# Signs of the weights through a two-slope activation, and written-out step lists, in an attention + feed-forward kernel on one core

## The chip, the core and the metric

The kernel runs on one core of one Trainium2 chip. The core has a matrix engine (PE), a vector engine (DVE), a scalar or activation engine (ACT), a third elementwise engine (POOL) and a queue of its own for issuing transfers (SP). Each of them executes its own instructions in program order and waits on semaphores of the others. The metric is the device time of one execution in microseconds; lower is better. The kernel before takes 952.94 us, the median of three runs (951.0 to 953.82).

## The reference

There are 8 batches of 8 heads with 512 local and 32 global tokens of 64 features. Local queries see the 32 global keys and the local keys at most 32 positions away; global queries see everything. The result, 512 features a token, goes through a feed-forward layer of 2048 hidden features.

```python
s_g = scale * np.matmul(q_g, k_all.transpose(0, 1, 3, 2))
out_g = np.matmul(sm(s_g), v_all)
s_ll = np.where(np.abs(pos[:, None] - pos[None, :]) <= 32, s_ll, -1e9)
a_l = sm(np.concatenate([s_lg, s_ll], axis=-1))
out_l = np.matmul(a_l, np.concatenate([v_g, v_l], axis=2))
x = np.concatenate([out_g, out_l], axis=2)   # then tokens x 512
h = x @ w_in                                 # 512 -> 2048
g = np.maximum(h, 0.0) + np.log1p(np.exp(-np.abs(h)))
out = g @ w_out                              # 2048 -> 512
```

## The kernel before

The weights lie in memory as 64-bit floats. Each of the 32 tiles (`wi0` to `wi15` of the first matrix, `wo0` to `wo15` of the second) arrives as two int32 words a number, `wiraw`/`woraw`, and passes three steps. **W** (`weight_mul`, L576, ACT) multiplies the high words, read as fp32, by 2^-112, which moves the exponent to fp32's bias. **B** or **b** (`weight_bits`, L581 to L583, DVE) shifts that word left by 3, puts the sign back and fills in three bits of the low word; B works in a PSUM bank (tag `a`), b in an SBUF tile. **H** or **h** (`weight_halves`, L588 on ACT and L589 on POOL for H, on DVE for h) splits the fp32 number into a high and a low fp32r half. The activations are split likewise (`xh`, `xl`, and `gh`, `gl`), and a product is three matmuls: high by high, high by low, low by high.

A feed-forward tile is 128 hidden features of a batch's 512 tokens, 16 tiles to a batch. `h` is 12 matmuls of 512 columns into one of two banks (tag `h`), written in two halves of 6. Then come Abs, Exp and Ln on ACT (L628 to L630), a max-and-add on DVE (`e`, L631), the cast `gh` on ACT (L634) and the difference `gl` on POOL (L635). `o` is 12 matmuls into four output banks, in two halves of 6.

Attention of batch 0 runs first, in eight groups of its heads, with its own layout: U steps in the lists below (scores `s`, sums, exps L200, diagonals, turned probabilities `t`, casts `p_..gh`/`p_..gl` L241 and L242, values `o`, and the split of x, L259 and L260). The global queries of batch 0 are two more groups (`s0g`, `t0g`, `p0g1gh` L284, `p0g1gl` L285, `o0g`). Later batches have four pairs of heads each, m = 4 to 31: scores `s_ps` (S with its mask added by PE matmuls and a copy on ACT L342, D with its mask added on DVE L340), maxima M (L343 to L401), products P on POOL or Q on DVE (L413, L415), exps E (L419), sums Z and R (`zt`, `rb`), values V (`v_ps`, and `xa` L466), X for the split. The `a` bank is used in turn by turned probabilities, B steps, `v_ps` and half of `s_ps`; the `h` banks also hold parts of `v_ps` and `s_ps` in steady batches.

The order on every engine is the order in which the program is written. Before, it comes from three tables: `START`, a list of steps for the time before the first feed-forward tile; `SLOTS`, four places of steps for each of batch 0's 16 tiles; and `S_AT`, `V_AT`, `PRE`, from which `later` and `moe_items` put the attention of the next batch between the tiles of the present one. Attention of batch b+1 thus runs among the feed-forward tiles of batch b; batch 7 has no attention beside it, and a last short pass (`GLOBAL` below) does the global tokens.

Of the kernel before, what the change touches and what calls it, by code (L numbers as in the profile page):

```python
# [8 lines left out]
F32 = mybir.dt.float32  # L9
# [4 lines left out]
ALU = mybir.AluOpType  # L14
# [17 lines left out]

M0 = 4
MLAST = 7
S_AT = (2, 4, 9, 11)
V_AT = (8, 15)
PRE = (3, 3)
START = (
# [4 lines left out]
)  # L43
SLOTS = (
    ('U65 B B M4 U66 H P41 P40', 'B', 'S50 H', 'W E41'),
    ('D51 E40 U93 W Z4 U94 B H', 'W', 'B B H', 'H M5 U95 W U96'),
    ('H', '', 'W', 'B R4 W'),
    ('', '', 'B', ''),
    ('W W B P51', 'B W', '', 'P50'),
    ('', 'E50', 'V4', 'B'),  # L50
    ('E51 H B W', '', 'Z5 S60', 'W h S61'),
    ('B B H W', 'W W B', 'h H', 'R5'),
    ('h', 'H', 'V5 M6', ''),
    ('', 'H W P60 D70', '', ''),
    ('B', '', 'D71', 'E60 P61 B H'),
    ('H B', 'E61 H M7 W', 'W W', 'P70 B Z6 W H'),
    ('H B', 'E70', '', 'H B R6 H'),
    ('', '', 'W P71', 'V6 B'),
    ('B h', '', 'H', ''),
    ('E71 Z7 W', '', 'B X0', 'H R7 X1 V7'),  # L60
)
GW = 76
W_PRE = 9
# [18 lines left out]
def moe_over_global_local_attention(  # L82
# [294 lines left out]
    def spread(mt):  # L377
        for a in range(1, 4):
            inorder(nc.gpsimd.tensor_copy(mt[0:32, GW * a:GW * a + GW], mt[32 * a:32 * a + 32, 0:GW]))
# [103 lines left out]
            if k < M:  # L483
                load_v(k)

    def step_of(o):

        kind, m, p = o[0], int(o[1:2] or 0), int(o[2:3] or 0)
        if kind in "SD":
            return [lambda: scores(m, p, kind == "D"), lambda: load(m + 1, p), *([lambda: spread(st["mt", m])] if p else [])]  # L490
        if kind == "V":
            return [lambda: values(m, a_banks(m)), lambda: values_out(m), lambda: load_v(m + 2)]
        if kind == "U":
            return [lambda: steps[m][0][p](*steps[m][1])]
        return {"M": [lambda: maxima(m), lambda: lift(m, 0), lambda: lift(m, 1)], "P": [lambda: probs(m, p, nc.gpsimd)],
                "Q": [lambda: probs(m, p, nc.vector)], "E": [lambda: exps(m, p)], "Z": [lambda: sums_first(m)],
                "R": [lambda: sums_rest(m)], "X": [lambda: split_x(1, m)], "K": [key_masks],
                "W": [weight_mul], "B": [lambda: weight_bits(True)], "b": [lambda: weight_bits(False)],
                "H": [lambda: weight_halves(nc.gpsimd)], "h": [lambda: weight_halves(nc.vector)]}[kind]

    def later():

        plan = {}

        def put(f, what, *fs):
            plan.setdefault((f // NF, f % NF, what), []).extend(fs)

        for f, slots in enumerate(SLOTS):
            for what, ops in zip(("pre", "act", "mid", "end"), slots):
                for o in ops.split():  # L510
                    put(f, what, *step_of(o))
        for m in range(MLAST + 1, M):
            b, i = divmod(m - 4, H // 2)
            at = NF * b + S_AT[i]
            put(at, "group", lambda m=m: scores_all(m), lambda m=m: spread(st["mt", m]))
            if m + 1 < M:
                put(at, "group", *[lambda m=m, p=p: load(m + 1, p) for p in range(NPC)])
            put(at + 1, "act", lambda m=m: maxima(m), *[lambda m=m, p=p: lift(m, p) for p in range(NPC)], lambda m=m: probs(m, 0, nc.gpsimd))
            put(at + 2, "act", lambda m=m: exps(m, 0), lambda m=m: probs(m, 1, nc.gpsimd))
            put(at + 3, "act", lambda m=m: exps(m, 1))  # L520
            if m % 2:
                at = NF * b + V_AT[i // 2]
                put(at - 1, "end", lambda m=m: sums_first(m))
                if i // 2:
                    put(at, "act", lambda b=b: split_x(b + 1, 0), lambda b=b: split_x(b + 1, 1))
                put(at, "act", lambda m=m: sums_rest(m))
                put(at, "group", lambda m=m: values_two(m - 1))
            else:
                put(at + 4, "act", lambda m=m: sums_first(m))
                put(at + 5, "act", lambda m=m: sums_rest(m))  # L530
        return plan

    halved = set()

# [38 lines left out]

    def abs_w(kind, k):
        hi = raws[kind, k][:, :, 1]
        note("act", nc.scalar.mul(hi.bitcast(F32), hi.bitcast(F32), DOWN))  # L576

    def bits_w(kind, k, r):
        t = raws.pop((kind, k))
        lo32, hi32 = t[:, :, 0], t[:, :, 1]  # L580
        note("dve", nc.vector.tensor_scalar(r, hi32, 3, None, op0=ALU.logical_shift_left))  # L581
        note("dve", nc.vector.scalar_tensor_tensor(r, hi32, -0x80000000, r, op0=ALU.bitwise_and, op1=ALU.bitwise_or))
        note("dve", nc.vector.scalar_tensor_tensor(lo32, lo32, 29, r, op0=ALU.logical_shift_right, op1=ALU.bitwise_or))  # L583
        return lo32.bitcast(F32)

    def halves_w(kind, k, r, engine):
# [10 lines left out]
    one = const.tile([P, 1], F32, name="one")  # L597
    nc.vector.memset(one, 1.0)

    def moe_items():  # L600


        tiles = [(b, f) for b in range(B) for f in range(NF)] + [(B, f) for f in range(NF // 2)]
        g, po, items = {}, {}, []

        def parts(b, f):

# [58 lines left out]
        halves = [(c, f, t) for c, f in tiles for t in range(0, 4 if c < B else 2, 2)]

        def second(i, at):
            c, f, t0 = halves[i]
            items.append((at, 2, 0, lambda: [opart(c, f, t) for t in (t0, t0 + 1)]))  # L670


        done, plan = 0, later()

        def run(fs):
            return lambda: [f() for f in fs]

        for i, (b, f) in enumerate(tiles):
            if f == 0 and b > 0:
                items.append((b, 0, 0, lambda b=b: [split_x(b, j) for j in range(4) if (b, j) not in halved]))  # L680
                second(done, b)
                done += 1
            w = 0 if b else 4 * f
            items.append((b, 2, w and w + 2, lambda b=b, f=f: hpart(b, f, (0, 1))))
            if (b, f, "pre") in plan:
                items.append((b, 0, 0, run(plan.pop((b, f, "pre")))))
            items.append((b, 2, w and w + 4, lambda b=b, f=f: (hpart(b, f, (2, 3)), act(b, f))))
            if (b, f, "act") in plan:
                items.append((b, 0, 0, run(plan.pop((b, f, "act")))))
            behind = 1 if ((b, f + 1) not in tiles and (b, f, 'group') not in plan) or (f == 0 and b > 0 and (b, 2, 'group') not in plan) else 2  # L690
            upto = halves.index(tiles[i - behind] + (0,)) + (2 if tiles[i - behind][0] < B else 1) if i >= behind else 0
            while done < upto:
                second(done, b)
                done += 1
                if (b, f, "mid") in plan:
                    items.append((b, 0, 0, run(plan.pop((b, f, "mid")))))
            if (b, f, "mid") in plan:
                items.append((b, 0, 0, run(plan.pop((b, f, "mid")))))
            if (b, f, "group") in plan:
                ahead = PRE[f in V_AT]  # L700
                for k in range(ahead - 2):
                    second(done, b)
                    done += 1
                items.append((b, 0, 0, run(plan.pop((b, f, "group")))))
                second(done, b)
                done += 1
            for what in ("max", "end"):
                if (b, f, what) in plan:
                    items.append((b, 0, 0, run(plan.pop((b, f, what)))))
        assert not plan, plan  # L710
        while done < len(halves):
            second(done, B)
            done += 1
        return items
# [55 lines left out]
    for o in START.split():
        for f in step_of(o):
            f()
    strict.append(1)
    items = moe_items()
    loads(W_PRE + 6)
    for b, size, w, it in items:
        if b == B - 1 and started:
            started.clear()  # L780
        it()
    assert wk[1] == len(order_w) and not todo and not done_bits
# [58 lines left out]
```

## Time and profile before

| | |
|---|---|
| median of three runs | 952.94 us |
| the profiled execution | 953.57 us, span 951.8 us |
| granted TensorE clock, mean | 0.995 |
| PE busy | 927.0 us, 97% |
| DVE, ACT, POOL busy | 589.9, 495.8, 452.4 us (62, 52, 48%) |
| PE's matmuls for h and o, of the chain that ended last | 37% and 37% of the span |

PE is busy nearly throughout, so the time is PE's work and the stretches in which it has none or runs at a lower clock. Both can be read from a table of windows: window less busy PE time is idle time; a granted clock below 1 stretches matmuls that count as busy.

### The profile page before, as it was taken

How to read it: one execution, taken by the hardware profiler on the slowest of the kernel's cores; microseconds unless marked ns; L12 is line 12 of the kernel's file. 1: busy time of each engine (PE TensorE's matmuls, PEld its weight loads, DVE VectorE, ACT ScalarE, POOL GpSimd, SP SyncE). 2: the span in 40 equal slices, each digit the busy share in tenths (PEclk: the TensorE clock that was granted, in tenths of full speed). 3: DMA queues.
4: the chain of work that ended last, by engine and by line, in shares of the span. 5: the costliest groups of instructions: out<-in, count | busy, mean ns of one | idle time of the engine just before them, and what ended most of it. 6: DMA issues, size and time to landing. Idle time of an engine off the chain costs nothing.

```text
span 951.8 us, 14719 instructions
## 1 busy us (share of the span) xinstructions
PE 927.0 (97%) x5465; PEld 766.2 (80%) x5468; DVE 589.9 (62%) x1197; ACT 495.8 (52%) x835; POOL 452.4 (48%) x672
## 2 busy tenths in 40 slices
PE   6899999999999999999999999999999999999997
PEld 4677786788888888888888888888888888888896
DVE  6889798667673767567684767466675757311211
ACT  5757666645364535634465535544455535544453
POOL 4346558445462727445462726444554636322221
PEclk9998999999999999999999999999999999999999
DMA  9546321120202121221211121211111010200000
GB/s 354 191 163 234 108 79 43 60 85 20 78 19 92 32 66 32 80 63 36 63 48 64 32 66 32 80 62 38 61 57 58 28 50 1 69 1 1 23 23 23
DMA packets 30697, 64.60 MB, mean 68 GB/s; under 512 B 7328, under 2 KB 7840, under 8 KB 30624
## 3 DMA queue, kind: packets, MB, share of 16 engines
q1 hardware_dynamic: 29888, 63.32, 20.0%
q8 instruction: 43, 0.70, 0.3%
q10 hardware_dynamic: 736, 0.33, 0.2%
q14 instruction: 30, 0.25, 0.1%
HBM read 54.20 MB, written 9.44 MB: 67 GB/s over the span
## 4 chain that ended last, share of the span: by engine, by line
PE 87%; DVE 4%; ACT 4%; POOL 2%; issue 2%; DMA 0%; ACTq 0%; POOLq 0%; DVEq 0%; SPq 0%
PE h L150 37%; PE o L150 37%; PE s_ps L150 6%; PE v_ps L150 5%; ACT e L200 1%; PE t L150 1%; PE s L150 1%; POOL wi L589 1%; DVE e L631 1%; DVE mt L343 1%; ACT e L630 1%; PE o0g L150 1%; DVE sums L197 1%; ACT e L629 1%; ACT e L628 0%
## 5 line engine op out<-in xcount | busy, mean ns | idle before, releaser
L150 PE MATMUL h<-xh,wi 128*128 128x512 f32 (+1 forms) x1152 | 342.1, 380 | 3.1 <-POOL wi L589 1.7
L150 PE MATMUL o<-wo,gh 128*128 128x512 f32 x1088 | 341.4, 395 | 0.2 <-POOL wo L589 0.2
L635 POOL TENSOR_TENSOR gl<-e,gh 128x512 fp32r<-128x512 f32 x136 | 175.4, 1290 | 317.5 <-ACT gh L634 228.0
L631 DVE SCALAR_TENSOR_TENSOR e<-h,e 128x512 f32<-128x512 f32 x136 | 92.9, 683 | 287.4 <-ACT e L630 281.1
L150 PEld LDWEIGHTS h<-xh,wi 128*128 128x128 f32 x1152 | 213.2, 189 | 45.8 <-POOL wi L589 2.5
L150 PEld LDWEIGHTS o<-wo,gh 128*128 128x128 f32 x1088 | 200.9, 188 | 44.4 <-POOL wo L589 0.5
L150 PE MATMUL h<-xl,wi 128*128 128x512 f32 (+1 forms) x576 | 218.3, 379 | 0.0
L150 PE MATMUL o<-wo,gl 128*128 128x512 f32 x544 | 211.8, 389 | 0.0
L628 ACT ACTIVATE e<-h 128x512 f32<-128x512 f32 x136 | 80.5, 592 | 227.5 <-PE h L150 189.7
L634 ACT CAST gh<-e 128x512 fp32r<-128x512 f32 x136 | 84.4, 621 | 131.8 <-DVE e L631 131.8
L150 PEld LDWEIGHTS h<-xl,wi 128*128 128x128 f32 x576 | 109.0, 189 | 20.4
L150 PEld LDWEIGHTS o<-wo,gl 128*128 128x128 f32 x544 | 102.3, 188 | 22.0
L413 POOL TENSOR_TENSOR s<-s,mb 128x768 f32<-128x768 f32 (+1 forms) x56 | 95.8, 1710 | 14.1 <-PE o L150 11.5
L630 ACT ACTIVATE e<-e,one 128x512 f32<-128x512 f32 x136 | 98.6, 725 | 4.4
L629 ACT ACTIVATE e<-e 128x512 f32<-128x512 f32 x136 | 86.0, 632 | 4.3
L419 ACT ACTIVATE s<-s 128x1024 f32<-128x1024 f32 x56 | 59.2, 1059 | 20.3 <-POOL s L415 20.3
L430 DVE TRANSPOSE_TENSOR_REDUCE zt<-s 128x32 f32<-128x1024 f32 x56 | 65.8, 1212 | 1.1 <-ACT s L419 1.1
L150 PE MATMUL s_ps<-raw 64*128 64x192 f32 (+2 forms) x672 | 63.5, 319 | 0.1
L150 PEld LDWEIGHTS s_ps<-raw 64*128 64x128 f32 x672 | 53.2, 187 | 9.8 <-issue 9.7
L368 DVE TRANSPOSE_TENSOR_REDUCE mt<-s 128x32 f32<-128x1024 f32 x48 | 56.7, 1219 | 0.0
L150 PEld LDWEIGHTS v_ps<-s,v 128*64 128x64 f32 x896 | 49.1, 137 | 8.8 <-issue 6.7
L150 PE MATMUL v_ps<-s,v 128*64 128x96 f32 (+3 forms) x896 | 54.1, 278 | 1.1 <-issue 1.1
(153 smaller groups left out, 833.2 us busy)
## 6 DMA issues: line engine op xcount, KB each, us to landing
raw<-in_qk SPq DMA_DIRECT2D x32, 352.0 KB, 3.0
v<-in_v SPq DMA_DIRECT2D x28, 384.0 KB, 3.2
raw<-in_qk SPq DMA_DIRECT2D x28, 368.0 KB, 3.7
wiraw<-in_w_in SPq DMA_DIRECT2D x16, 512.0 KB, 8.9
woraw<-in_w_out SPq DMA_DIRECT2D x16, 512.0 KB, 8.6
out<-ot SPq DMA_DIRECT2D x32, 256.0 KB, 2.1
v<-in_v SPq DMA_DIRECT2D x4, 512.0 KB, 8.7
raw<-in_qk SPq DMA_DIRECT2D x4, 416.0 KB, 8.3
```

What stands on the lines that cost most here:

```text
L150: order["pe"] = after(nc.tensor.matmul(*a, **k), "pe").ins
L197: keep("dve", nc.vector.tensor_reduce(t[:, 0, 0:n], ps, axis=AX.X, op=ALU.max))
L368: inorder(nc.vector.tensor_reduce(windows(mt, 4 + 16 * p, 36, 2, 16), st["s", m, p].rearrange("p h (b k) -> p h b k", k=32), axis=AX.X, op ...
L413: inorder(engine.tensor_tensor(sw, sw, pairs(mb, 352, mo, md, w), op=ALU.subtract))
L419: inorder(nc.scalar.activation(s, s, AF.Exp, scale=0.125))
L430: inorder(nc.vector.tensor_reduce(windows(zt, 4 + 16 * p, 36, 2, 16), st["s", m, p].rearrange("p h (b k) -> p h b k", k=32), axis=AX.X, op ...
L628: inorder(nc.scalar.activation(e, ph, AF.Abs))
L629: inorder(nc.scalar.activation(e, e, AF.Exp, scale=-1.0))
L630: inorder(nc.scalar.activation(e, e, AF.Ln, bias=one))
L631: inorder(nc.vector.scalar_tensor_tensor(e, ph, 0.0, e, op0=ALU.max, op1=ALU.add))
L634: inorder(nc.scalar.copy(gh, e))
L635: inorder(nc.gpsimd.tensor_tensor(gl, e, gh.bitcast(F32), op=ALU.subtract))
```

## The change

First, `abs_w` uses a parametric ReLU instead of a multiplication: the scale is 2^-112 as before, and negative words are multiplied by 2^32 besides. That puts a bit into them which the later shift by 3 moves to the sign's place. `bits_w` then needs two DVE instructions instead of three. Second, the tables and the two functions that read them are replaced by four lists: `OPENING` (batch 0's attention, the weights, batch 0's 16 tiles and batch 1's attention), `STEADY` for each of batches 1 to 6, `LAST` and `GLOBAL`. In them `h` is a tile's first half, `g` its second half and the activation, `o` two output rows; N is what H was. In the listing of the changed program line numbers are one higher through the attention and five or six higher from the weights' steps on.

```diff
-START = (
-    "U00 U10 U01 W U11 K U02 U12 U20 U03 b U04 H W U30 b U21 U31 U13 U22 U14 H W U05 "
...
-SLOTS = (
-    ('U65 B B M4 U66 H P41 P40', 'B', 'S50 H', 'W E41'),
...
+OPENING = (
+    "U00 K U10 U01 U11 U02 U12 W U20 b U03 U04 N W U30 U13 b U21 U22 U14 W U40 b U05 U23 U31 "
...
+STEADY = (
+    "x2 x3 o h g h g o h g o o o S0 o h g M0 P00 h o g P01 o E00 o "
+    "S1 E01 o h g M1 P10 h g E10 P11 o h Z0 o g o E11 o Z1 h R0 o g R1 o "
...
-        note("act", nc.scalar.mul(hi.bitcast(F32), hi.bitcast(F32), DOWN))
+        note("act", nc.scalar.activation(hi.bitcast(F32), hi.bitcast(F32), AF.Prelu, scale=DOWN, alpha=2.0 ** 32))
...
-        note("dve", nc.vector.tensor_scalar(r, hi32, 3, None, op0=ALU.logical_shift_left))
-        note("dve", nc.vector.scalar_tensor_tensor(r, hi32, -0x80000000, r, op0=ALU.bitwise_and, op1=ALU.bitwise_or))
-        note("dve", nc.vector.scalar_tensor_tensor(lo32, lo32, 29, r, op0=ALU.logical_shift_right, op1=ALU.bitwise_or))
+        note("dve", nc.vector.tensor_scalar(r, lo32, 29, None, op0=ALU.logical_shift_right))
+        note("dve", nc.vector.scalar_tensor_tensor(lo32, hi32, 3, r, op0=ALU.logical_shift_left, op1=ALU.bitwise_or))
...
+        def ff_first():
+            hpart(*tiles[count["h"]], (0, 1))
+            count["h"] += 1
+        def ff_second():
+            hpart(*tiles[count["g"]], (2, 3))
+            act(*tiles[count["g"]])
+            count["g"] += 1
+        def ff_out():
+            c, f, t0 = halves[count["o"]]
+            for t in (t0, t0 + 1):
+                opart(c, f, t)
+            count["o"] += 1
...
+    for o in OPENING.split():
+        if o == "h" and not strict:
+            strict.append(1)
+        step_of(o, 0)
+    for b in range(1, B - 1):
+        for o in STEADY.split():
+            step_of(o, b)
```

The lists move instructions on all engines. On PE, at the end of batch 0's own attention, the values of the second group of global queries (`o0g1`) stand before between the last half of `h0_1` and `h0_2`:

```order
L150 MATMUL h0_1_788<-xh0_3_674,wi1_308 128x512 x2
L150 MATMUL h0_1_788<-xl0_3_675,wi1_308 128x512
L150 MATMUL o0g1_884<-p0g1gh_830,v0_2_125 128x64 x4
L150 MATMUL o0g1_884<-p0g1gl_831,v0_2_125 128x64
L150 MATMUL o0g1_884<-p0g1gh_830,v0_3_135 128x64 x4
L150 MATMUL o0g1_884<-p0g1gl_831,v0_3_135 128x64
L150 MATMUL h0_2_902<-xh0_0_354,wi2_362 128x512 x2
```

and now:

```order
L151 MATMUL h0_1_761<-xl0_3_634,wi1_356 128x512
L151 MATMUL o0_0_858<-wo0_539,gh0_0_754 128x512 x2
L151 MATMUL o0_0_858<-wo0_539,gl0_0_755 128x512
L151 MATMUL o0_1_862<-wo0_539,gh0_0_754 128x512 x2
L151 MATMUL o0_1_862<-wo0_539,gl0_0_755 128x512
L151 MATMUL o0_2_866<-wo0_539,gh0_0_754 128x512 x2
L151 MATMUL o0_2_866<-wo0_539,gl0_0_755 128x512
L151 MATMUL o0_3_870<-wo0_539,gh0_0_754 128x512 x2
L151 MATMUL o0_3_870<-wo0_539,gl0_0_755 128x512
L151 MATMUL o0g1_874<-p0g1gh_820,v0_2_125 128x64 x4
```

The 12 output matmuls of tile 0, which stood behind `h0_2`, now stand ahead of `o0g1`.

On POOL, among batch 0's tiles 10 to 12, the low halves of `wi12` and `wi13` stand before with that of `wo10` between them:

```order
L415 TENSOR_TENSOR s6_1_1211<-s6_1_1211,mb6_1_1364 128x2x96
L589 TENSOR_TENSOR wi12_1491<-wiraw12_1017,wi12_1491 128x512
L589 TENSOR_TENSOR wo10_1501<-woraw10_1045,wo10_1501 128x512
L635 TENSOR_TENSOR gl0_11_1519<-e0_11_1513,gh0_11_1518 128x512
L589 TENSOR_TENSOR wi13_1523<-wiraw13_1140,wi13_1523 128x512
```

and now:

```order
L416 TENSOR_TENSOR s6_1_1198<-s6_1_1198,mb6_1_1336 128x2x96
L594 TENSOR_TENSOR wi12_1459<-wiraw12_996,wi12_1459 128x512
L640 TENSOR_TENSOR gl0_11_1478<-e0_11_1472,gh0_11_1477 128x512
L594 TENSOR_TENSOR wi13_1518<-wiraw13_1175,wi13_1518 128x512
L414 TENSOR_TENSOR s7_0_1356<-s7_0_1356,mb7_0_1502 128x2x2x160
```

`wo10`'s difference is now on DVE, and `wi13` comes one instruction earlier.

On PE in a steady batch (here batch 2), before, `v_ps12` is followed by an output half of `wo7`, the whole tile `h2_9`, an output half of `wo8` and then the scores of m = 14; this is the end of it:

```order
L150 MATMUL h2_9_3371<-xh2_3_2846,wi9_1233 128x512 x2
L150 MATMUL h2_9_3371<-xl2_3_2847,wi9_1233 128x512
L150 MATMUL o2_0_2942<-wo8_1302,gh2_8_3279 128x512 x2
L150 MATMUL o2_0_2942<-wo8_1302,gl2_8_3280 128x512
L150 MATMUL o2_1_2946<-wo8_1302,gh2_8_3279 128x512 x2
L150 MATMUL o2_1_2946<-wo8_1302,gl2_8_3280 128x512
L150 MATMUL s_ps14_0_3399<-raw14_0_3112 128x160 x2
```

and now:

```order
L151 MATMUL v_ps12_1_3325<-s12_1_2949,v12_2801 64x192 x2
L151 MATMUL v_ps12_1_3325<-s12_1_2949,v12_2801 64x96 x2
L151 MATMUL o2_0_2907<-wo8_1222,gh2_8_3250 128x512 x2
L151 MATMUL o2_0_2907<-wo8_1222,gl2_8_3251 128x512
L151 MATMUL o2_1_2911<-wo8_1222,gh2_8_3250 128x512 x2
L151 MATMUL o2_1_2911<-wo8_1222,gl2_8_3251 128x512
L151 MATMUL s_ps14_0_3364<-raw14_0_3077 128x160 x2
```

`h2_9` and the rest of `wo7` moved ahead of `v_ps12`; one output half is left between `v_ps12` and the scores.

## Rows read from the trace of the kernel before

**Rows 1.** The page's first part: busy time, share of the span, instructions of each engine.
```profile
PE 927.0 (97%) x5465; PEld 766.2 (80%) x5468; DVE 589.9 (62%) x1197; ACT 495.8 (52%) x835; POOL 452.4 (48%) x672
```
**Rows 2.** Windows of the span: length, busy time of each engine, PEclk, DMA, GB/s.
```profile
5.00:55.00 50.00, 43.34 (x362) 34.17 (x364) 39.75 (x86) 32.48 (x101) 18.58 (x19) 1.00 0.63 239
55.00:82.00 27.00, 23.82 (x154) 19.06 (x152) 25.05 (x42) 16.75 (x30) 17.25 (x25) 0.87 0.82 299
82.00:145.00 63.00, 62.84 (x355) 50.54 (x354) 54.72 (x103) 42.34 (x66) 33.69 (x44) 1.00 0.27 92
145.00:155.00 10.00, 7.69 (x25) 5.35 (x24) 9.73 (x20) 7.57 (x12) 8.67 (x12) 0.83 0.00 0
175.00:185.00 10.00, 8.79 (x61) 6.95 (x60) 8.35 (x22) 4.96 (x12) 6.17 (x8) 1.00 0.25 82
185.00:945.00 760.00, 758.03 (x4402) 632.49 (x4401) 433.89 (x883) 376.77 (x593) 350.92 (x530) 1.00 0.15 46
```
**Rows 3.** PE's timeline, 10 to 60 us: start, duration, instruction, [idle before, releaser].
```profile
17.62 2.00 PE L150 MATMUL t<-diag(0, 1)_232,e 128*128 128x128 f32 x16 [1.95 <-DVE p_0gl L242]
45.42 1.13 PE L150 MATMUL s0g<-raw,raw 128*128 128x256 f32 x4 [1.55 <-ACT e L200]
```
**Rows 4.** DVE's and ACT's timelines, 27 to 42 us.
```profile
29.73 0.45 ACT L200 ACTIVATE e<-s,sums 128x224 f32<-128x224 f32 x1 [1.80 <-DVE wbitswi L581]
39.46 0.69 DVE L582 SCALAR_TENSOR_TENSOR wbitswo<-woraw,wbitswo 128x512 int32<-128x512 int32 x1
41.06 0.17 DVE L206 TENSOR_SCALAR sums<-sums 128x4 f32<-128x4 f32 x1 [0.18 <-ACT e L200]
```
**Rows 5.** PE's timeline around `o0g1`, 73 to 78 us.
```profile
73.24 1.10 PE L150 MATMUL o0g<-p0g1gh,v 128*128 128x64 f32 x8 [1.27 <-ACT p0g1gh L284]
74.79 0.69 PE L150 MATMUL o0g<-p0g1gl,v 32*128 32x64 f32 x2 [0.44 <-DVE p0g1gl L285]
75.40 1.97 PE L150 MATMUL o0g<-p0g1gh,v 128*128 128x64 f32 x8
```
**Rows 6.** Windows of 5 us around that place.
```profile
70.00:75.00 5.00, 3.29 (x18) 2.33 (x18) 4.93 (x6) 4.17 (x8) 4.71 (x12) 0.94 1.03 385
75.00:80.00 5.00, 5.00 (x17) 4.26 (x18) 4.77 (x8) 2.77 (x5) 3.51 (x5) 0.50 1.03 409
```
**Rows 7.** PE's timeline at 149.6 and 177.6 us, POOL's at 148.3 us.
```profile
149.62 0.79 PE L150 MATMUL h<-xh,wi 128*128 128x512 f32 x1 [1.27 <-POOL wi L589]
177.60 2.03 PE L150 MATMUL v_ps<-s,v 128*64 128x160 f32 x32 [1.06 <-issue]
148.28 1.29 POOL L589 TENSOR_TENSOR wi<-wiraw,wi 128x512 fp32r<-128x512 f32 x1
```
**Rows 8.** Groups by line: count, busy, mean ns of one, idle before and releaser.
```profile
L582 DVE SCALAR_TENSOR_TENSOR wbitswi<-wiraw,wbitswi 128x512 int32<-128x512 int32 x13 | 9.7, 750 | 0.4
L582 DVE SCALAR_TENSOR_TENSOR wbitswo<-woraw,wbitswo 128x512 int32<-128x512 int32 x12 | 8.3, 696 | 0.4
L576 ACT ACTIVATE woraw<-woraw 128x512 f32<-128x512 f32 x16 | 10.9, 681 | 3.7 <-DMA woraw<-in_w_out 3.7
L106 ACT ACT_TABLE_LOAD x1 | 1.3, 1283 | 0.7 <-PEq L832 0.7
L150 PE MATMUL s_ps<-raw,raw 64*128 64x32 f32 x112 | 11.4, 244 | 2.0 <-DVE e L631 2.0
```
**Rows 9.** SP's queue: one issue at 54.87 us; the page's group of all such transfers.
```profile
54.87 0.43 SPq L566 DMA_DIRECT2D woraw<-in_w_out  x1
woraw<-in_w_out SPq DMA_DIRECT2D x16, 512.0 KB, 8.6
```
**Rows 10.** Timelines of DVE and PE behind `v_ps` in a steady batch.
```profile
236.33 1.58 DVE L466 TENSOR_TENSOR xa<-v_ps,rb 128x384 f32<-128x384 f32 x4
232.55 3.83 PE L150 MATMUL v_ps<-s,v 128*64 128x160 f32 x64
237.82 0.63 PE L150 MATMUL h<-xh,wi 128*128 128x512 f32 x2
```

More of the change, by code (lines that the diff above doesn't have):

```diff
@@ L34 @@
 MLAST = 7
-S_AT = (2, 4, 9, 11)
-V_AT = (8, 15)
-PRE = (3, 3)
-START = (
[4 rows of a table removed]
-)
-SLOTS = (
-    ('U65 B B M4 U66 H P41 P40', 'B', 'S50 H', 'W E41'),
[L46 to L60, printed above, removed]
+OPENING = (
[11 rows of a table added]
+)
+STEADY = (
[4 rows of a table added]
+)
+LAST = (
[3 rows of a table added]
+)
+GLOBAL = (
+    "x0 x1 x2 x3 o h g o h g h g o h g o h g o h g o h g o h "
+    "g o o o "
 )
@@ L484, in values_two, with step_of @@
                 load_v(k)
-    def step_of(o):
+    def step_of(o, b):
         kind, m, p = o[0], int(o[1:2] or 0), int(o[2:3] or 0)
+        if kind in "hgo":
+            return {"h": ff_first, "g": ff_second, "o": ff_out}[kind]()
+        if b and kind in "SMPQEZRV":
+            m += 4 * b + 4
         if kind in "SD":
[L490 to L527, printed above, removed]
-            else:
-                put(at + 4, "act", lambda m=m: sums_first(m))
-                put(at + 5, "act", lambda m=m: sums_rest(m))
-        return plan
@@ new lines, in step_of @@
+            if b:
+                scores_all(m)
+                spread(st["mt", m])
+                for k in range(NPC if m + 1 < M else 0):
+                    load(m + 1, k)
+            else:
+                scores(m, p, kind == "D")
+                load(m + 1, p)
+                if p:
+                    spread(st["mt", m])
+        elif kind == "V":
+            if b:
+                values_two(m)
+            else:
+                values(m, a_banks(m))
+                values_out(m)
+                load_v(m + 2)
+        elif kind == "U":
+            steps[m][0][p](*steps[m][1])
+        elif kind == "M":
+            maxima(m)
+            for k in range(NPC):
+                lift(m, k)
+        elif kind in "PQ":
+            probs(m, p, nc.gpsimd if kind == "P" else nc.vector)
+        elif kind == "E":
+            exps(m, p)
+        elif kind == "Z":
+            sums_first(m)
+        elif kind == "R":
+            sums_rest(m)
+        elif kind == "X":
+            split_x(b + 1, m)
+        elif kind == "x":
+            split_x(b, m)
+        elif kind == "K":
+            key_masks()
+        elif kind == "W":
+            weight_mul()
+        elif kind in "Bb":
+            weight_bits(kind == "B")
+        else:
+            weight_halves(nc.gpsimd if kind == "N" else nc.vector)
@@ L598, in moe_over_global_local_attention @@
     nc.vector.memset(one, 1.0)
-    def moe_items():
-        tiles = [(b, f) for b in range(B) for f in range(NF)] + [(B, f) for f in range(NF // 2)]
-        g, po, items = {}, {}, []
+    tiles = [(b, f) for b in range(B) for f in range(NF)] + [(B, f) for f in range(NF // 2)]
+    halves = [(c, f, t) for c, f in tiles for t in range(0, 4 if c < B else 2, 2)]
+    g, po, count = {}, {}, {"h": 0, "g": 0, "o": 0}
+    if True:
         def parts(b, f):
@@ L664, in store @@
                     (nc.scalar if i % 2 else nc.sync).dma_start(out=out[r:r + SG, :], in_=o[SG * i:SG * i + SG])
[L666 to L714, printed above, removed]
+        def ff_first():
[10 more added lines that the diff above has]
+            count["o"] += 1
@@ L771, in moe_over_global_local_attention @@
     started.append(1)
[L772 to L782, printed above, removed]
+    for o in OPENING.split():
[5 more added lines that the diff above has]
+            step_of(o, b)
+    started.clear()
+    for b in range(B - 1, B + 1):
+        for o in (LAST if b < B else GLOBAL).split():
+            step_of(o, b)
+    assert wk[1] == len(order_w) and not todo and not done_bits and count["o"] == len(halves)
 def _layout(q_l, k_l, v_l, q_g, k_g, v_g):
```

18 rows, old and new, of tables (LAST, OPENING, START, STEADY) are left out of this document.

## The prediction

> **What bounds the kernel now.** I read the page's busy times first. PE works 927.0 us of a span of 951.8 [rows 1], and no other engine comes near, so the time is PE's work, plus what PE idles, plus what it loses at a lower clock. The second view is the table of windows, in which these two losses can be placed [rows 2]. Idle is the window less PE's busy time; the clock's loss I take as the window times one minus PEclk. From 5 to 55 us PE idles 6.7 us; from 55 to 82 us 3.2 us, and the clock of 0.87 costs 27 x 0.13 = 3.5; from 82 to 145 us 0.2; from 145 to 155 us 2.3 and, at 0.83, 1.7; from 175 to 185 us 1.2; from 185 to 945 us 2.0 in all. Together some 21 us, of which about 17 lie in the first 155 us, while batch 0 and the weights are worked on. The steady batches can hardly be improved: 2.0 us in 760.
>
> The third view is PE's timeline at these places. In the first 55 us PE waits in turn for DVE's or ACT's part of an attention group, 1.95 us for a cast at 17.6 and 1.55 us for exps at 45.4 [rows 3]; such rows repeat for the ten groups. At 73 us it waits 1.27 and 0.44 us for the turned probabilities of the second global group [rows 5]. The 5 us before hold only 3.29 us of PE work, and in the next 5 the granted clock is 0.50, the lower of its two levels, 1.2 GHz [rows 6]: the same 8 matmuls of `o0g` take 1.97 us instead of 1.10 [rows 5]. At 149.6 us PE waits 1.27 us for the low half of `wi13` on POOL, at 177.6 us 1.06 us for `v_ps` [rows 7].
>
> **The change part by part.**
>
> *Two instructions for the bits.* L582 goes 32 times: 13 at 750 ns and 19 at 696 [rows 8], where one of the three groups of 19 stands, 9.7 + 13.2 = 22.9 us of DVE. DVE gains an addition of a mask, three halves of weights and one product that others did before, about 0.7 to 1.3 us each by the like instructions, so 18 us are left. None of this is on the path by itself, since DVE is 62% busy. It counts where PE waits for a DVE result that stands behind a weight step. In the first 55 us both cases are in the trace. At 29.7 ACT waited 1.80 us for sums behind a weight step on DVE; but at 41.1 DVE itself waits 0.18 us for ACT's exps directly behind such a step [rows 4], so the step lay wholly beside the exps, and a shorter one only lengthens DVE's wait.
>
> *The parametric ReLU* takes the place of an ACTIVATE of 681 ns, 32 of them [rows 8], with the same shape. No row shows this function. Its cost I take as that of the multiplication, so 0 in the sum. For the upper bound I let it run at half the rate: an exp of 224 columns took 0.45 us [rows 4] and the multiplication of 512 took 0.68, which is 0.8 ns a column and 0.27 fixed, so half the rate adds 0.41 us, 13 us in all on an engine that is idle 48% of the time; the lower bound is 0. The program before has one table load, of 1283 ns [rows 8]; the changed order holds one, too. The Trainium skill ("ScalarE: Activation LUTs", section "Table sets: the hidden batching unit" and "Same chain, other wiring" before it) says that a function outside the active set needs a load ahead of it, and that the wiring by which a parametric ReLU picks its slope is not reachable from a kernel. By the second rule the negative slope would do nothing, and the time would be the same; by the first it is the fourth rival below. No row of before shows either.
>
> *Order, 5 to 55 us* (6.7 us idle). Scores of the next group stand ahead of values of the last in several places, and DVE's steps are shorter. Against it: a group's exps are a serial chain on ACT that nothing shortens. The gain is between −2 and 6.7; I take 2.5, for the waits like that at 29.7 go and those like that at 41.1 stay.
>
> *Order, 55 to 82 us* (6.7 us). The 12 output matmuls of tile 0 are now ahead of `o0g1`. Half a tile's output lies in a steady batch between `v_ps`'s end, 232.55 + 3.83 = 236.38, and the next `h` at 237.82 [rows 10], 1.4 us; so they are 2.8 us of work and fill the wait of 1.27 + 0.44. DVE's chain before the second cast is one step of 0.70 shorter besides. Without that gap I expect the clock to stay at the upper level, which gives back the 2.5 us of 75 to 80 us [rows 6]. The Trainium skill ("TensorE: Matmul & The Clock Gate", "HAM oscillation") puts it as a rule that gaps in PE's work bring the half clock for the work behind them; the two windows agree with it, and by it the whole 3.5 would come back. Two hazards stand against this: three weight multiplications now wait ahead of tile 0's Abs on ACT, and their transfers are issued in one row from 54.87 us and take 8.6 us as a mean [rows 9], with the DMA share at 1.03 [rows 6]; and if they make tile 0's `gh` late, the gap stands ahead of `o0_0` in place of `o0g1`, and only the step of 0.70 is won, about 1. Bounds 1 and 6.2; I take 5, nearer to the end at which the matmuls fill the gap, since several other matmul groups stand between `h0_0` and `o0_0`.
>
> *Order, 82 to 145 us*: 0.2 idle, so nothing.
>
> *Order, 145 to 155 us* (4.0). The difference of `wo10`, 1.3 us, leaves POOL between `wi12` and `wi13`, DVE has most of the 18 us less work behind it, and `h0_12`'s second half stands later. The wait of 1.27 should go, and the low clock around it. Bounds 0 and 3.7; I take 3.
>
> *175 to 185 us* (1.2). `v_ps` waits for the bank in which the bits of `wo15` are worked out; that chain is one step of 0.69 shorter, and it starts earlier. Bounds 0 and 1.3; I take 1.
>
> *Steady batches.* The 2.0 us that `s_ps` waits for `e` [rows 8], six times 0.33, have another tile's `e` in front of them now. But `s_ps` of m = 4b + 6 stands only one output half, 6 matmuls or 1.4 us, behind `v_ps`; it needs the bank that `xa` reads for 1.58 us from `v_ps`'s end [rows 10], so a wait of 0.1 to 0.2 us appears, which two output halves and a whole tile, about 5.6 us, covered before. Sum 6 x (0.33 − 0.13) = 1.2, bounds −2 and 2. Two mask matmuls of 512 columns turn into an addition on DVE: by six in 1.4 us, 0.5.
>
> Sum: 2.5 + 5 + 0 + 3 + 1 + 1.2 + 0.5 = 13.2 us. A tighter order has small waits of its own that I can't place; for ten groups at 0.2 us I take off 2. That leaves 11.2 of the profiled execution's 953.57, so 942.4; that execution stands 0.6 above the median, so **942** us against 952.94.
>
> **The rivals.**
>
> *The opening is bound by ACT's chain and by transfers*, so that DVE's saving is hidden. For it: DVE's wait at 41.1, the DMA share of 1.03, the 8.6 us of a transfer. Then 5 to 55 gives 0, 55 to 82 about 1, and the rest 145 to 155 at 2 and the steady batches at 1: 4 us, **949**. Against it: ACT's wait of 1.80 behind a weight step [rows 4], and that `wo0`'s matmuls fill a gap whatever else is late.
>
> *Everything goes*: all idle time and all clock loss up to 185 us but some 2 us, 6.7 + 6.2 + 3.7 + 1.2 + 1.7 less 2: 17.5, **936**. For it: the work that can be put into the gaps is there. Against it: the ten groups' serial exps.
>
> *Slower: the bank behind `v_ps`.* The place is `s_ps` of every steady batch, one output half behind `v_ps`. If `rb`, which `xa` needs, comes late, because DVE's reduction waits for POOL's gather behind the other pair's sums, `s_ps` stands by that much. It decides from the point at which `xa` ends more than 1.4 us behind `v_ps`: each 1.5 to 3 us are paid six times, 9 to 18 us, and with clock loss behind such a gap more. Net of the opening's gain of 4 to 11 that is 953 to 962, **957**. Against it: `rb` was there at 236.3, when `v_ps` ended, so that `xa` began at once [rows 10].
>
> *The table loads.* If the new function stood in another table set than Exp and Ln, each of 32 weight multiplications could bring two loads, 64 x 1.28 = 82 us on ACT, half of it or more seen by PE in the first 180 us: **1000** or above. The Trainium skill's rule on table sets, named above, is this rival's ground; the changed program's one load speaks against it.
>
> **How the numbers follow.** The forecast, 938 to 946, has 0.56; the bound opening, 946 to 950.5, 0.22; everything goes, below 938, 0.10; no measurable change, by several of the small waits, 0.06; the bank, 0.05; the table loads, 0.01. What a measurement of this kernel tells from no change is 0.3%, 2.9 us, so faster means below 950.1: 0.56 + 0.10 + nearly all of 0.22, 0.87; the same 0.08; slower 0.05. The range of 8 in 10 leaves about one tenth on each side: 934 to 950.
>
> **What would show it.** In the profile after, PE should have no wait before `o0g1`, PEclk 1.00 from 70 to 85 us and from 145 to 155; these two give most. PE's idle time up to 55 us should be about 4 us instead of 6.7. In the weight steps DVE shows two instructions, the ACTIVATE still about 0.68 us. In the steady batches a wait of `s_ps` for `xa` of 0.1 to 0.2 us and a batch's length unchanged within 0.3 us. I am wrong if the low clock of 75 to 80 us is still there, or if it only moves; if a wait for a weight's transfer stands ahead of tile 0's Abs and PE's gap is now ahead of `o0_0`; or if `s_ps` waits over 1 us in every steady batch.

## The result and the profile after

The changed kernel takes 936.98 us (median; 936.88 to 937.54, four runs), the one before 953.38 beside it: a ratio of 0.983, 95% interval 0.982 to 0.984, or 16.4 us less. The forecast was 942, range 934 to 950. The profiled execution is one of 936.9 us, span 935.1.

The page's first part, and the table of windows (columns as in [rows 2]) with the same bounds as before:

```profile
PE 919.9 (98%) x5466; PEld 761.7 (81%) x5466; DVE 578.6 (62%) x1172; ACT 496.3 (53%) x834; POOL 445.5 (48%) x666
```
```profile
5.00:55.00 50.00, 45.33 (x382) 36.12 (x381) 35.40 (x80) 31.57 (x100) 15.33 (x15) 1.00 0.62 238
55.00:82.00 27.00, 25.54 (x160) 20.65 (x159) 24.76 (x45) 19.25 (x34) 16.78 (x25) 1.00 0.90 321
82.00:145.00 63.00, 63.00 (x355) 50.43 (x354) 57.34 (x102) 46.63 (x74) 39.50 (x46) 1.00 0.26 83
145.00:155.00 10.00, 10.00 (x68) 8.15 (x67) 9.09 (x22) 6.58 (x11) 9.02 (x14) 1.00 0.40 128
175.00:185.00 10.00, 10.00 (x64) 8.30 (x62) 2.89 (x4) 6.02 (x10) 3.90 (x4) 1.00 0.15 54
185.00:930.00 745.00, 744.95 (x4336) 621.43 (x4334) 433.52 (x880) 371.54 (x581) 346.19 (x526) 1.00 0.15 46
```

Against [rows 2]: the granted clock is 1.00 in every window, and from 82 to 930 us PE idles less than 0.1 us. The last 5.1 us of the span hold 0.24 us of PE work, much as before (1.60 of the last 6.8). What is left of other waits lies in the first 70 us. PE's timeline has these there, the largest behind the first scores (start, duration, instruction, idle before and releaser), against [rows 3]:

```profile
17.62 2.00 PE L151 MATMUL t<-diag(0, 1)_231,e 128*128 128x128 f32 x16 [1.00 <-DVE p_0gl L243]
27.27 2.00 PE L151 MATMUL t<-diag(1, 1)_364,e 128*128 128x128 f32 x16 [0.81 <-DVE sums L207]
43.25 1.47 PE L151 MATMUL t0g<-diag,e_g 128*128 128x128 f32 x10 [1.67 <-DVE p_1gl L243]
59.91 0.73 PE L151 MATMUL h<-xh,wi 128*128 128x512 f32 x2 [0.79 <-ACT yg L302]
66.00 1.47 PE L151 MATMUL t0g<-diag,e_g 128*128 128x128 f32 x10 [0.64 <-DVE wiraw L588]
...
73.41 1.00 PE L151 MATMUL o0g<-p0g1gh,v 128*128 128x64 f32 x8
```

The last row is `o0g1`, which has no wait and runs at the full clock, against [rows 5]. The first row is no gain, though it shows 1.00 us and [rows 3] 1.95: both begin at 17.62 us. E11 below has the same lists up to there, and its trace shows the longer wait:

```profile
17.52 2.00 PE L149 MATMUL t<-diag(0, 1)_231,e 128*128 128x128 f32 x16 [1.95 <-DVE p_0gl L241]
```

So a recorded wait, and PE's busy time with it (45.33 us from 5 to 55 us here, 43.73 in E11), can differ by 1 to 2 us between executions that do the same work.

Windows move when a program gets shorter, and recorded waits differ, so the gain is divided at marks: the starts of PE rows by which both programs have done the same work, but for the mask matmuls that the change took away. The marks are the first `h`, the row behind both `h0_2` and `wo0`'s outputs, and the first scores of batch 1's and of batch 2's list. Before:

```profile
58.08 0.73 PE L150 MATMUL h<-xh,wi 128*128 128x512 f32 x2 [0.79 <-DVE xl L260]
...
59.58 1.00 PE L150 MATMUL o0g<-p0g0gh,v 128*128 128x64 f32 x8
...
62.26 0.73 PE L150 MATMUL h<-xh,wi 128*128 128x512 f32 x2
...
85.03 0.61 PE L150 MATMUL h<-xh,wi 128*128 128x512 f32 x2
...
195.19 1.14 PE L150 MATMUL s_ps<-raw 64*128 64x160 f32 x12
...
300.46 1.14 PE L150 MATMUL s_ps<-raw 64*128 64x160 f32 x12
```

After (the first `h` is the row at 59.91 above):

```profile
79.03 0.62 PE L151 MATMUL o<-wo,gh 128*128 128x512 f32 x2
...
182.90 1.14 PE L151 MATMUL s_ps<-raw 64*128 64x160 f32 x12
...
287.43 1.14 PE L151 MATMUL s_ps<-raw 64*128 64x160 f32 x12
```

Up to the first `h`: `o0g0` (62.26 − 59.58 = 2.68 us) now stands ahead of it, so 60.76 compares with 59.91, a gain of 0.85. The mask matmuls that are gone stood here, so their 0.5 us is part of it. In E4 to E7, whose lists are the same up to this mark, the first `h` begins at 59.13 to 59.95 us, so the gain is 0.8 to 1.6 by the execution. To the second mark 85.03 − 79.03 = 6.00, so 5.15 of its own. To batch 1's scores 110.16 against 103.87, 6.29. A steady batch 105.27 against 104.53, 0.74; if all six are alike, 4.4. Together 16.7, the difference of the spans.

The activation costs what the multiplication did (681 ns), and there is one table load. Its negative slope acts, which the prediction left open: the weights' signs come from nothing else.

```profile
L582 ACT ACTIVATE woraw<-woraw 128x512 f32<-128x512 f32 x16 | 10.8, 678 | 2.5 <-DMA woraw<-in_w_out 2.5
L107 ACT ACT_TABLE_LOAD x1 | 1.3, 1283 | 0.7 <-PEq L801 0.7
```

### The profile page after: what moved, and what is told of

The parts are those of the page before. It is cut to its first block, busy times and chain, and to the rows that moved or that the text cites. A ratio compares the mean times of both kernels' runs of the same rounds, so it can differ in the third digit from the quotient of the medians.

```text
span 935.1 us, 14695 instructions
## 1 busy us (share of the span) xinstructions
PE 919.9 (98%) x5466; PEld 761.7 (81%) x5466; DVE 578.6 (62%) x1172; ACT 496.3 (53%) x834; POOL 445.5 (48%) x666
## 4 chain that ended last, share of the span: by engine, by line
PE 94%; DVE 3%; ACT 2%; issue 1%; POOL 0%; ACTq 0%; POOLq 0%
PE o L151 41%; PE h L151 39%; PE s_ps L151 7%; PE v_ps L151 6%; ACT e L201 1%; PE s L151 1%; PE t L151 1%; DVE sums L198 1%; PE t0g L151 0%; PE o0g L151 0%; PE s0g L151 0%; DVE p_1gl L243 0%; DVE wbitswo L587 0%; DVE mb L402 0%; DVE sums L199 0%
## 5 line engine op out<-in xcount | busy, mean ns | idle before, releaser
L414 POOL TENSOR_TENSOR s<-s,mb 128x640 f32<-128x640 f32 (+1 forms) x55 | 94.0, 1709 | 16.2 <-DVE mb L402 9.7
L380 POOL COPY mt<-mt 32x76 f32<-32x76 f32 x84 | 20.1, 239 | 83.9 <-DVE mt L369 72.5
```

The source lines that it names most:

```text
L414: inorder(engine.tensor_tensor(sw, sw, pairs(mb, 352, mo, md, w), op=ALU.subtract))
```

## The experiments

Times are medians; the ratio is to the kernel before on the same chip (953.3 to 953.9 us), with its 95% interval, and "less" is worked out from the ratio. Differences to the changed kernel's 936.98 us are between medians. Letters of steps are those of the lists. One more difference goes with the lists, whichever an experiment uses: the program before issues the transfers of some weights at one point ahead of the first feed-forward tile, and the changed one has no such step. The issues there begin at 54.87 us before and at 54.54 in the changed kernel; this was not tried by itself.

**E1, the bits alone.** The lists of before, and these two edits:

```diff
-        note("act", nc.scalar.mul(hi.bitcast(F32), hi.bitcast(F32), DOWN))
+        note("act", nc.scalar.activation(hi.bitcast(F32), hi.bitcast(F32), AF.Prelu, scale=DOWN, alpha=2.0 ** 32))
...
-        note("dve", nc.vector.tensor_scalar(r, hi32, 3, None, op0=ALU.logical_shift_left))
-        note("dve", nc.vector.scalar_tensor_tensor(r, hi32, -0x80000000, r, op0=ALU.bitwise_and, op1=ALU.bitwise_or))
-        note("dve", nc.vector.scalar_tensor_tensor(lo32, lo32, 29, r, op0=ALU.logical_shift_right, op1=ALU.bitwise_or))
+        note("dve", nc.vector.tensor_scalar(r, lo32, 29, None, op0=ALU.logical_shift_right))
+        note("dve", nc.vector.scalar_tensor_tensor(lo32, hi32, 3, r, op0=ALU.logical_shift_left, op1=ALU.bitwise_or))
```

> The order of before, with the parametric ReLU and the two-instruction bits alone: 32 DVE instructions of 0.70 to 0.75 us fewer, 22.9 us. Theory 1 (the steps' lengths matter little, the order brings the gain): the 0.60 us wait of t0g1 and parts of the waits at 146 to 150 and 177 us get shorter, 2 to 4 us in all, 949 to 951 us, with the low clock behind o0g1 still there. Rival (the shorter DVE work is what brings it): the waits before o0g1 and at 146 to 150 us go by themselves, with the clock, 10 us or more, 943 or below. A third: DVE reaches its waits on ACT sooner and nothing changes, 953.

951.83 us, ratio 0.998 (0.997 to 0.999), 1.8 us less. The waits before `o0g1` and for `wi13` are no shorter than before (1.27 and 0.44, 1.27 us), and they are behind ACT and POOL too:

```profile
72.43 1.10 PE L150 MATMUL o0g<-p0g1gh,v 128*128 128x64 f32 x8 [1.08 <-ACT p0g1gh L284]
74.45 0.43 PE L150 MATMUL o0g<-p0g1gl,v 32*128 32x64 f32 x2 [0.91 <-DVE p0g1gl L285]
...
148.31 0.79 PE L150 MATMUL h<-xh,wi 128*128 128x512 f32 x1 [1.62 <-POOL wi L588]
```

So shorter DVE steps by themselves don't remove them. Theory 1 held in kind; its 2 to 4 us were not quite reached.

**E2, the lists alone.** The changed program with the old multiplication and the old three instructions (the edits of E1 undone).

> The new lists with the old multiplication and the old three instructions for the bits. Theory 1: most of the gain stays, 12 to 14 of 16.4 us, 939 to 942 us; the waits in the first 60 us and at wi13 grow by some tenths to 1 us each. Rival: the new order needs the shorter DVE steps, since o0g1, h0_12 and v_ps7 stand closer behind weights now; then waits and low clock come back in the first 150 us and 946 us or more is measured, with only the steady batches' gain of 4.4 us and little else left.

951.04 us, ratio 0.997 (0.996 to 0.998), 3.1 us less instead of 12 to 14. Theory 1 fell. The rival held, and more than held: 4.4 us of gain are the steady batches' (E5 and E6), so the opening list with the old steps is about 1 us slower than that of before. The window from 82 to 145 us, two of PE's waits in it, and DVE ahead of the second:

```profile
82.00:145.00 63.00, 58.37 (x324) 46.09 (x325) 58.76 (x104) 40.89 (x68) 32.22 (x37) 0.97 0.32 110
```
```profile
100.51 2.03 PE L151 MATMUL v_ps<-s,v 128*64 128x160 f32 x32 [0.85 <-DVE wiraw L589]
...
112.84 0.39 PE L151 MATMUL s_ps<-mask,ident 128*128 128x512 bf16 x1 [1.90 <-DVE woraw L589]
```
```profile
110.64 0.69 DVE L587 TENSOR_SCALAR wbitswo<-woraw 128x512 int32<-128x512 int32 x1
111.37 0.69 DVE L588 SCALAR_TENSOR_TENSOR wbitswo<-woraw,wbitswo 128x512 int32<-128x512 int32 x1
112.10 0.69 DVE L589 SCALAR_TENSOR_TENSOR woraw<-woraw,wbitswo 128x512 int32<-128x512 int32 x1
```

DVE works 58.76 of 63 us, and PE waits for a bank in which weight bits are still worked out. The changed program has 63.00 us of PE work in that window, and before it was 62.84. So the lists bring work forward for which DVE has time only with the shorter steps. This is not all of it. E2's profile is of an execution of 953.21 us, above the median; its granted clock is 0.93 from 5 to 55 us, 0.94 from 55 to 82 and 0.97 from 82 to 145, which costs 3.5 + 1.6 + 1.9 = 7.0 us, against some 10 us more idle time than in the changed kernel. How much of the clock's part is the edit's and how much the execution's is open (see the last section).

No row of this kernel waits for `wi12` or `wi13`, but that does not show the wait cured: PE comes there 6 us later than before, and waits 1.08 us just ahead, for the half of `wo10` on DVE:

```profile
154.16 0.50 PE L151 MATMUL o<-wo,gh 128*128 128x512 f32 x1 [1.08 <-DVE wo L595]
```

The half of `wi13` ends on POOL at 155.30 us, and its matmuls begin at 155.42.

**E3, one move in the lists of before.** `wo0`'s outputs ahead of `o0g1` (H of before written N):

```diff
-N N M5 U95 W U96 h N g o W o B R4
+N N o o M5 U95 W U96 h N g W B R4
```

> The program of before with one move: the 12 output matmuls of tile 0 (wo0) stand ahead of o0g1 instead of behind the first halves of h0_2. Theory 1 (a gap filled and the clock kept): the waits of 1.27 and 0.44 us before o0g1 go, the granted clock of 70 to 85 us stays 1.00, 4 to 5 us less, 948.5 us. Rival (DVE's chain must be shorter, too): p0g1gl is later than the 2.7 us of matmuls reach, a wait of 0.5 to 1 us is left and the clock drops all the same, 951 to 953 us. A second rival (the low clock has nothing to do with the gap): 1.7 us less, 951.5, with PEclk about 0.5 somewhere in 70 to 85 us.

951.82 us, ratio 0.998 (0.997 to 0.999), 1.8 us less. The place itself did what theory 1 said; then the gain was given back:

```profile
75.00:80.00 5.00, 5.00 (x29) 4.21 (x29) 4.77 (x8) 2.75 (x5) 3.52 (x5) 1.00 1.03 407
```
```profile
81.05 0.73 PE L146 MATMUL h<-xh,wi 128*128 128x512 f32 x2 [0.62 <-ACT yg L297]
98.17 2.03 PE L146 MATMUL v_ps<-s,v 128*64 128x160 f32 x32 [1.85 <-DVE woraw L584]
```

The first row is at clock 1.00 where [rows 6] have 0.50. In the second fence PE, some 4 us earlier than before, stands at `v_ps4` for weight bits, a wait that before did not have.

**E9, both.** The lists of before with the edits of E1 and E3.

> The lists of before with two of the three edits: the two-instruction bits, and wo0's matmuls ahead of o0g1. Alone the one measured 1.9 us less, the other 1.9. Theory (moved work gains only where DVE is not late behind it: with wo0 moved alone PE waited 1.85 us for a weight's bits at v_ps4 and 0.62 for yg, as the gain of 5 us was partly given back): together more than the sum, 6 to 7 us less, 947 us, with PEclk 1.00 from 55 to 82 us and no wait behind bits from 82 to 145. Rival (the two add up): 3.8 us less, 950.

946.11 us, ratio 0.993 (0.992 to 0.995), 6.4 us less (7.2 by the medians) where the two alone make 3.6. PE's timeline has no wait from 58 to 140 us. Theory held.

**E4, that move undone in the changed program.**

```diff
-g N W o o U95 N M5 h U96 B B g B R4
+g N W U95 N M5 h U96 B B g o o B R4
```

> The changed program with the one move undone: wo0's 12 output matmuls stand behind h0_2 again. Theory 1: the wait of some 2.5 us comes back before o0g1 (its casts end 2.7 us behind the end of h0_1 in the changed program), and the low clock behind it costs another 1 to 3.5 us: 939.5 to 942.5 us. Rival (the gap is what costs, the clock doesn't drop): 938.5 to 939.5 with PEclk 1.00. Rival 2 (DVE's shorter chain makes o0g1 ready early): 937.

941.17 us, ratio 0.987 (0.985 to 0.989), 4.2 us above the changed kernel's 936.98. The waits are back, and the low clock behind them:

```profile
72.84 1.10 PE L149 MATMUL o0g<-p0g1gh,v 128*128 128x64 f32 x8 [1.51 <-ACT p0g1gh L283]
74.56 0.43 PE L149 MATMUL o0g<-p0g1gl,v 32*128 32x64 f32 x2 [0.61 <-DVE p0g1gl L284]
```
```profile
75.00:80.00 5.00, 4.77 (x18) 3.90 (x19) 4.84 (x14) 3.42 (x8) 4.26 (x5) 0.67 1.03 392
```

2.1 us of wait, and the window's lower clock, 5 x 0.33 = 1.7. The profile has another 1.7 us of low clock from 55 to 65 us (0.96 and 0.70), ahead of the moved matmuls; E5 and E6 have it too, without this edit, so it is not put down to the edit.

**E5 and E6, the steady list.** E5 is the changed program with the steady batches' order of before; E6 changes one place of that, `h` of tile 9 ahead of `v_ps`:

```diff
-R1 o o o V0 o h g o S2
+R1 o o o h g o V0 o S2
```

> The changed program with the steady list of before in batches 1 to 6. The trace of before shows a wait of 0.33 us of s_ps for e in each of them; the distance from one batch's first scores to the next is 105.27 us before and 104.53 after. Theory 1 (the batch's order alone makes this, and the true wait is the 0.73 us by which the stretch from one s_ps to the next is longer, the row shows only part of it): 6 x 0.73 = 4.4 us more, 941.4 us. Rival (0.33 us is all that the order brings, the rest is another effect, such as the state of transfers or the shorter DVE work): 2.0 us more, 939.0.

> As the kernel with the old steady list, with one place changed: h_9 and its output half ahead of v_ps, so that one output half stands between v_ps and the scores of m = 4b + 6. Theory 1 (the one place is all): 937.0 us, as the changed program. Rival (other moves in the list share the gain): 938 to 941. Second rival (the bank that xa reads is late here): a new wait of s_ps of 0.1 to 0.2 us a batch, 938.

E5: 940.99 us, ratio 0.987 (0.985 to 0.988), 4.0 more than the changed kernel. E6: 936.60, ratio 0.982 (0.981 to 0.984), the changed kernel's time, and 4.4 less than E5 on the same chip. So one place in a list is the whole of the steady gain, and a row that shows 0.33 us (E5's is the same as before) stood for 0.7:

```profile
231.41 0.29 PE L150 MATMUL s_ps<-raw,raw 64*128 64x32 f32 x1 [0.33 <-DVE e L635]
```

The second rival, the wait for `xa` that the prediction counted too, isn't there. In the changed program:

```profile
224.34 3.83 PE L151 MATMUL v_ps<-s,v 128*64 128x160 f32 x64
...
229.71 1.14 PE L151 MATMUL s_ps<-raw 64*128 64x160 f32 x12
```
```profile
227.57 1.81 DVE L467 TENSOR_TENSOR xa<-v_ps,rb 128x384 f32<-128x384 f32 x4 [1.68 <-PE v_ps L151]
```

`xa` begins 0.6 us ahead of `v_ps`'s end (224.34 + 3.83 = 228.17), with the part that is finished, and ends at 229.38, before the scores.

**E7 and E10, `wo10`'s difference.** E7 puts it back on POOL in the changed program (`M7 n W` to `M7 N W`), E10 puts it on DVE in E9 (`h N B g E61` to `h n B g E61`).

> The changed program with the difference of wo10 on POOL instead of DVE, at the same place of the list, ahead of wi13's as before. wi13's half ends at 141.58 us and its matmuls begin at 141.71, so theory 1: they wait about 1.2 us, and with a low clock behind it up to 2 us more: 938.2 to 940.2 us. Rival (DVE being earlier is what cured this place, POOL has slack): 937.0.

> As the kernel with the two edits in the old lists, and wo10's difference on DVE as well. Theory: POOL's order is what holds up wi13 at 146 to 150 us, but wi13's POOL step still has the activation's difference and ACT's cast ahead of it, which ends 0.9 us before POOL began; so the wait of 1.6 us falls to 0.7, and with a shorter low clock 1 to 2 us less than without it, 945 to 946 us. Rival (wo10 alone held it up): no wait and clock 1.00, 3.5 to 4 us less. Second rival (only h0_12's second half behind an output half hides it): less than 0.5 us.

E7: 937.86 us, ratio 0.984 (0.982 to 0.986), 0.9 more, which the intervals don't tell from the changed kernel; PE waits 0.17 us for `wo10` and not for `wi13`. The 1.2 us and more that theory 1 wanted are not there. E10: 946.36, ratio 0.994 (0.992 to 0.995), as E9. Its waits, against 0.47, 0.21 and 1.64 us in E9:

```profile
141.46 0.50 PE L146 MATMUL h<-xh,wi 128*128 128x512 f32 x1 [0.91 <-POOL wi L589]
143.54 0.51 PE L146 MATMUL h<-xh,wi 128*128 128x512 f32 x1 [0.64 <-ACT wi L588]
144.92 0.50 PE L146 MATMUL h<-xh,wi 128*128 128x512 f32 x1 [0.88 <-POOL wi L589]
```

2.43 us against 2.32. The wait for `wi13` is halved, those ahead of it grow. The place of `wo10` is not what held PE up: the theory and its first rival were off. The time is what the second rival said (less than 0.5 us), by which `h0_12`'s second half behind an output half hides the wait; that place was not tried by itself.

**E8, E11, E12, what is left.** E11 moves `yg`'s copies (U66), E8 also the scores of the second global group (U90) to the front, E12 puts `t0g0` (U63) behind them instead. The edit of all three, that of E8, that of E12:

```diff
-U65 W U85 W U86 U66 h
+U65 W U85 U66 W U86 h
```
```diff
-U35 U45 W U36 U63 U46 N U72 U64 n U90 b
+U90 U35 U45 W U36 U63 U46 N U72 U64 n b
```
```diff
-U35 U45 W U36 U63 U46 N U72 U64 n U90 b
+U35 U45 W U36 U46 N U72 U90 U63 U64 n b
```

> An attempt at the largest waits that are left. The copies of the first global group's output (yg, L302) stand ahead of the split of the last local group and of one weight multiplication, for the 0.79 us that h0_0's bank waits for them; and the scores of the second global group stand ahead of the third group's last steps and of t0g0, which waits 1.67 us. Theory 1: both waits are filled, 934.5 to 935.5 us. Rival (the waits move to the next step of the same chain of exps and casts): 936.5 to 937.5. Worse, if the moved scores wait for their bank and hold up t0g0: 938.

> The changed program with the copies of the first global group's output (yg) ahead of a weight multiplication and of the last local group's split, without the other move that was tried with it. Theory: h0_0's bank is free 0.5 us or more earlier, the wait of 0.79 us goes, and 0.5 to 0.8 us are won, 936.3 us. Rival (tile 0's activation waits for its weights' transfers on ACT and t0g1 for bits, which takes the gain back): 937.0.

> As the kernel with the yg move, and t0g0 behind the scores of the second global group, whose 2.2 us of matmuls fill t0g0's wait of 1.67 us; the third group's chain keeps its place ahead of them. Theory: 1.2 to 1.7 us less, 935 us. Rival (those scores wait for their own bank or the chain of the last local group gets later by their sums on DVE, as with the move that was tried before): 937 or more.

E8: 940.02 us, ratio 0.986 (0.984 to 0.988), 3 worse. E11: 936.19, ratio 0.983 (0.981 to 0.984). E12: 937.01, ratio 0.983 (0.982 to 0.985). E11's wait at the first `h` is gone, the next at `t0g1` grew; its median is 0.8 lower, which the intervals don't tell from the changed kernel. In E8 and E12 a wait moved, and the clock fell besides: 0.97 from 5 to 55 us in E8, 0.83 from 55 to 65 in E12, some 1.5 and 1.7 us.

```profile
48.51 2.95 PE L149 MATMUL t<-diag(3, 0)_554,e 128*128 128x128 f32 x16 [3.54 <-POOL diag(3, 0)_554 L212]
```
```profile
46.73 2.00 PE L149 MATMUL t<-diag(3, 0)_536,e 128*128 128x128 f32 x16 [1.57 <-DVE p0g0gl L284]
```

The first is E8's: POOL's diagonal stands behind half a weight, whose cast stands behind the moved exps on ACT. The second is E12's: 1.57 us at the next user of the `a` bank in place of 1.67 at `t0g0`.

## Why the prediction came out as it did

The time fell in the range, on the gainful side, by 5 us more than forecast: outside the 938 to 946 to which the prediction gave 0.56. By its terms, at the marks above:

- *Bits, nothing by themselves*: right; 1.8 us (E1). That about 18 us of DVE would be left was too much: DVE's busy time fell from 589.9 to 578.6, 11.3. The product that moved to DVE takes 4 us, not 0.7 to 1.3, most of it while POOL works (last section). And I named DVE's 62% as cover; where the weights are worked on it was 54.72 of 63 us [rows 2], 87%. There the shorter steps are what lets the lists work: alone 3.1 and 1.8 us, together 16.4. The prediction added its terms and never asked if the order needs the bits; E2 shows that it does. Its terms for the order came near only because both edits were made together, and that is luck.
- *5 to 55 us, 2.5*: over; 0.85, of which 0.5 is the masks' (0.8 to 1.6 over executions). PE's recorded idle time fell to 4.7 us, near the 4 that I named as a sign, but the same matmuls have 6.3 us of it in E11: most of that sign is the recording.
- *55 to 82 us, 5*: right in mechanism and size; 5.15, and 4.2 when undone (E4), of which 3.8 is the wait and the low clock at that place. Its condition, DVE being less late behind it, is shown by E3 and E9.
- *82 to 185 us, 3 + 1*: under; 6.29, because all idle time and all clock loss went. The mechanism I named, `wo10` leaving POOL, failed: E10 wins nothing, and E7's 0.9 is within the noise. E9, with the shorter steps and `wo0` moved, still has the waits for `wi12` and `wi13`, and the changed program has none, so the rest of the order cures them. The row that goes with it is `h0_12`'s second half behind an output half, at 141.71 us, just behind `wi13`'s half on POOL; that I read in the trace and did not test by itself.
- *Steady batches, 1.2*: right place, size off; 4.4, and a batch is 0.74 us shorter where I said unchanged within 0.3. The 2.0 us of the row were a lower bound, and the new wait for `xa` that I took off doesn't exist: I read `xa`'s start at `v_ps`'s end [rows 10] as waiting for it, while `xa` had waited for DVE's own `rb`, which ended at 236.40 (235.59 + 0.81).
- *2 us off for small waits*: not seen; from 82 us on there are none.

Of the rivals, "everything goes" (936) was nearest, at a chance of 0.10; its reservation about the first 55 us was right. The opening bound by transfers did not come: in the changed kernel ACT waited 0.27 and 0.62 us for weights' transfers ahead of tile 0's Abs, but PE had no wait at `o0_0`. The bank behind `v_ps` and the table loads did not come either: one load, and E1 is no slower.

## What to carry to other kernels

Two edits that each look useless, one that shortens an off-path engine's steps and one that reorders work, can each be the other's condition: read the off-path engine's load in the stretch concerned, not over the span, and time them together before dropping either. A recorded wait is not its price, and one profile's busy and idle times can shift by a microsecond or two with nothing changed; the distance between two like marks, one with the wait and one without, gives the price. When a wait is filled, look for the next user of the same bank or engine, since that is where it went in three of the experiments (E3, E8, E12).

## What the runs showed of the hardware

The granted clock does not follow from a gap alone. E1 and E9 have the same three waits ahead of `wi12` and `wi13` (0.47, 0.20, 1.62 and 0.47, 0.21, 1.64 us) and the same PE work in the 10 us around them, first E1, then E9:

```profile
142.00:152.00 10.00, 7.70 (x25) 5.36 (x24) 8.66 (x18) 7.77 (x13) 9.70 (x15) 0.83 0.00 0
```
```profile
137.00:147.00 10.00, 7.68 (x32) 5.47 (x31) 8.72 (x18) 8.75 (x15) 9.85 (x13) 1.00 0.00 0
```

The clock fell in one and not in the other. Those are two programs, but the same happens with the same instructions. Up to the first `h` the changed kernel and E6 have the same lists, and both wait there 0.79 us for the same copy. In the changed kernel the two matmuls behind that wait take 0.73 us (the row at 59.91 above), in E6 1.22:

```profile
59.13 1.22 PE L150 MATMUL h<-xh,wi 128*128 128x512 f32 x2 [0.79 <-ACT yg L301]
```

In E6 the granted clock is 0.89 from 55 to 60 us and 0.77 from 60 to 65, some 1.7 us, and in the changed kernel 1.00. So part of what a filled gap gives back differs between executions; what decides stays open.

A product on DVE is slow beside a product on POOL. The one that moved to DVE, in the changed kernel, and POOL at that time:

```profile
92.21 0.95 DVE L414 TENSOR_TENSOR s<-s,mb 128x768 f32<-128x768 f32 x1
93.07 2.96 DVE L416 TENSOR_TENSOR s<-s,mb 128x64 f32<-128x64 f32 x2
```
```profile
93.02 1.28 POOL L640 TENSOR_TENSOR gl<-e,gh 128x512 fp32r<-128x512 f32 x1 [2.62 <-ACT gh L639]
94.26 1.56 POOL L414 TENSOR_TENSOR s<-s,mb 128x640 f32<-128x640 f32 x1
```
```profile
L416 DVE TENSOR_TENSOR s<-s,mb 128x192 f32<-128x192 f32 x1 | 1.7, 1730 | 0.0
L416 DVE TENSOR_TENSOR s<-s,mb 128x64 f32<-128x64 f32 x1 | 1.3, 1309 | 0.0
```

The 768 columns take 950 ns while POOL is idle; then 64 columns take 1309 and 192 take 1730, and each ends 0.1 to 0.2 us behind one of POOL's two instructions (94.30 and 95.82 us). E2 has the same: 948 ns with POOL idle, 1310 and 1749 from POOL's start at 101.79 on. It reads as DVE held up by POOL; no run tried it.
